# Strassen's seven products for the way up of two couples of blocks in the second MoE of a fused attention and MoE kernel

## The chip, the cores and the metric

One Trainium2 chip, one core of it. The metric is the device time of one execution in microseconds (us), the median of several runs.

## The reference

Attention with a causal mask and a forget bias feeds a gated MoE of one expert, and its result a second one; no step between them leaves the chip. What the change touches is the second:

```python
def _moe2_ref(x, w_in, w_out):      # x: 2304 x 512, w_in: 512 x 2048, w_out: 2048 x 512
    h = x @ w_in
    g = h - np.tanh(h)
    return (g @ w_out).astype(np.float32)
```

All of it is float32. The kernel keeps that precision on float16 operands: each operand is split into a high half (float16) and a low half (the rest, float16), and a product is three matmuls, high by high, high by low and low by high (`mm3`).

## The kernel before, in words

The 2304 tokens are cut into 6 blocks of 384 (`NBLK`, `TB`). Attention runs first, the first MoE of block j beside the attention of the next, and then the second MoE alone, block after block: for j in 0 to 5, 16 slices of 128 hidden columns on the way up (`up2`), then 4 parts of 128 output columns on the way down (`down2`). A slice on the way up is 4 pieces of 128 inputs by `mm3`, so 12 matmuls of 128 x 128 by 128 x 384, into one PSUM tile of `mm_tile` (4 of them in turn, tag `m2`). Then ScalarE takes the tanh (L1114), VectorE the difference of h and tanh h (L1115, which frees the PSUM tile), ScalarE copies it into the high half `DH` (L1116), and VectorE makes the low half `DL` (L1117). A part on the way down is 16 pieces by `mm3`, 48 matmuls, then an eviction on ScalarE (L1128) and a store.

The matmuls of all of them are the lines of `mm3`: L681, L682, L683. Weights come as 64-bit words that VectorE turns into float32 (`decode`, L547 to L549), ScalarE squares for their scale (L238), and `split` turns into halves (L563 on ScalarE, L564 on VectorE). These steps are a list of tasks (`w2_tasks`), run bit by bit in the last block of the first MoE and in block 0 of the second. A block's input is loaded as `x2f` and made into halves `x2h`, `x2l` by `x2_prep` (L1068, L1078, L1079).

The order on each engine is not the order of the code: the tile framework's scheduler moves instructions of one engine past each other where their data allow. On an engine they then run strictly in that order. `st_m1`, `st_m2` and the like are stacks of pools, closed when their memory goes to another.

Of the kernel before, what the change touches and what calls it, by code (L numbers as in the profile page):

```python
# [21 lines left out]
NBLK = 6  # L22
# [18 lines left out]
def tile_forget_attention_moe_moe2(ctx, tc, qa, qb, kt, va, vb, va0, vb0, s, wg, wv, wo, rg, win, wo2, out):  # L41
# [61 lines left out]
        return p.tile([128, 512], dtype, name=tag, tag=tag)  # L103

    wide = [None]

    def mm_tile():
# [878 lines left out]
    wide[0] = ps_x  # L986
# [4 lines left out]
    wt2 = {}  # L991

    def w2_tasks():
# [41 lines left out]
        def o_chain(g):
            ps = ps_x.tile([128, 512], FP32, name="px", tag="px")
            ones_sum(ps, wt2["ss"], 4)
            nm = small(const, [128, 1], FP32, f"nmo{g}")
            V.tensor_reduce(out=nm, in_=ps[:, 0:4], op=ALU.add, axis=AX.X)
            p2(nm, iso[:, g:g + 1], so[:, g:g + 1])  # L1040

        def o_conv(g, k):
            split(W2, 4 * g + k, so[:, g:g + 1])

        for key, piece, chain, conv in (("i", in_piece, in_chain, in_conv), ("o", o_piece, o_chain, o_conv)):
            for g in range(4):
                for k in range(4):
                    tasks.append(lambda g=g, k=k, piece=piece: piece(g, k))
                tasks.append(lambda g=g, chain=chain: chain(g))
                for k in range(4):  # L1050
                    tasks.append(lambda g=g, k=k, conv=conv: conv(g, k))
            if key == "i":
                tasks.append(lambda: V.tensor_reduce(out=wt2["si"], in_=si, op=ALU.min, axis=AX.X))
        return tasks

    x2s = {}

    def x2_load(j):
        t = x2_p.tile([128, 4, TB], FP32, name="x2f", tag="x2f", bufs=1)
        SY.dma_start(out=t, in_=x2d[j])  # L1060
        x2s[j] = t

    def x2_prep(j):
        t = x2s.pop(j)
        xh = x2_p.tile([128, 4, TB], FP16, name="x2h", tag="x2h")
        xl = x2_p.tile([128, 4, TB], FP16, name="x2l", tag="x2l")
# [10 lines left out]
        V.reciprocal(out=isd, in_=sd)  # L1077
        A.activation(out=xh, in_=t, func=ACTF.Copy, scale=sx)  # L1078
# [23 lines left out]

    st_m2 = ctx.enter_context(ExitStack())
    d_p = pool(st_m2, "d", bufs=1)
    t2_p = pool(st_m2, "t2", bufs=4)
    def up2(j, f, DH, DL):
        xh, xl, u, sd, _ = x2s[j, "p"]
        o = slice(128 * (f % 4), 128 * (f % 4) + 128)
        ps = mm_tile()
        for k in range(4):  # L1110
            mm3(ps, slot_h(WI, 4 * (f // 4) + k)[:, o], slot_l(WI, 4 * (f // 4) + k)[:, o], xh[:, k, :], xl[:, k, :], k, k == 0, k == 3)
        flush_moe()
        t = t2_p.tile([128, TB], FP32, name="t2", tag="t2")
        A.activation(out=t, in_=ps, func=ACTF.Tanh, scale=u[:, f // 4:f // 4 + 1])  # L1114
        V.scalar_tensor_tensor(out=t, in0=ps, scalar=u[:, f // 4:f // 4 + 1], in1=t, op0=ALU.mult, op1=ALU.subtract)  # L1115
        A.activation(out=DH[:, f, :], in_=t, func=ACTF.Copy, scale=sd)  # L1116
        moe_pend.append(lambda: V.scalar_tensor_tensor(out=DL[:, f, :], in0=t, scalar=sd, in1=DH[:, f, :], op0=ALU.mult, op1=ALU.subtract))  # L1117

    def down2(j, d, DH, DL):
# [4 lines left out]
        for k in range(16):  # L1124
            n, o = 4 * d + k // 4, slice(128 * (k % 4), 128 * (k % 4) + 128)
            mm3(ps, slot_h(W2, n)[:, o], slot_l(W2, n)[:, o], DH[:, k, :], DL[:, k, :], k, k == 0, k == 15)
        t = t2_p.tile([128, TB], FP32, name="t2", tag="t2")
        A.activation(out=t, in_=ps, func=ACTF.Copy, scale=io)  # L1128
        SY.dma_start(out=out[j, d], in_=t)

    for j in range(NBLK):
        DH = d_p.tile([128, 16, TB], FP16, name="dh", tag="dh")
        DL = d_p.tile([128, 16, TB], FP16, name="dl", tag="dl")
        for f in range(16):
            up2(j, f, DH, DL)
            if j == 0:
                run_tasks(w2t, -(-(nt - n5) // 14))
        if j == 0:
            run_tasks(w2t, 1000)
            st_ws.close()  # L1140
        if j + 1 < NBLK:
            x2_prep(j + 1)
            if j + 2 < NBLK:
                x2_load(j + 2)
        for d in range(4):
            down2(j, d, DH, DL)
    for st in (st_m2, st_w2):
        st.close()


# [49 lines left out]
```

## Time and profile before

| | |
|---|---|
| runs of the kernel | 1079.31, 1079.76, 1075.13 us; median 1079.31 |
| profiled execution | 1077.7 us, its span 1076.0 us |
| TensorE | busy 986.0 us, 92% of the span |
| VectorE, ScalarE, GpSimd | 621.3, 606.5 and 268.9 us |
| mean granted TensorE clock | 0.978 of 2.4 GHz |

In the profile PE is TensorE's matmuls, PEld its loads of weights, DVE VectorE, ACT ScalarE, POOL GpSimd and SP the engine that issues the DMAs. PEclk is the granted clock, 1.00 for 2.4 GHz. Matmuls overlap in their pipeline, so their durations add up to more than the time they take; the distance from one start to the next is what one costs. L1115 is line 1115 of the kernel before; the lines of the changed one are higher (L1254 there is L1115 here, L1256 is L1117, L1128 became L1269).

### The profile page before, as it was taken

The page shows a single profiled execution, that of the slowest core. Times are in us where ns is not written, and L with a number is a line of the kernel's source. Part 1 is how long each engine was busy: PE and PEld are TensorE (multiplying, and loading weights), DVE is VectorE, ACT ScalarE, POOL GpSimd, SP SyncE. Part 2 cuts the span into 40 slices and gives each one's busy share as a digit, 9 for nine tenths or more (in the row PEclk, how much of TensorE's full clock was granted, in tenths as well). Part 3 has the DMA queues.
Part 4 walks back from the last instruction along what each step waited for, and adds up shares of the span by engine and source line. Part 5 has one row for each costly group of instructions (what it writes and reads, how often), then busy time and mean ns, then how long its engine had stood idle before and what let it go on. Part 6 is the DMA issues. An engine that isn't in the chain of part 4 may idle for free.

```text
span 1076.0 us, 19457 instructions
## 1 busy us (share of the span) xinstructions
PE 986.0 (92%) x7575; PEld 626.7 (58%) x7576; DVE 621.3 (58%) x1445; ACT 606.5 (56%) x1194; POOL 268.9 (25%) x377
## 2 busy tenths in 40 slices
PE   1488977799899999999999899999999999999998
PEld 1376644455566666666666556666666666666665
DVE  8987998975585640673453988395442606243250
ACT  6589667776665662867667456465442516243240
POOL 5121265513462451455355112000000000000000
PEclk9986979999999999999999999999999999999999
DMA  8615524240202201301101950141010010100000
GB/s 271 251 36 123 177 87 125 64 140 30 66 22 60 54 17 67 90 12 27 55 12 39 339 172 13 48 156 45 16 37 23 5 55 2 45 15 9 23 1 30
DMA packets 49439, 76.82 MB, mean 71 GB/s; under 512 B 25890, under 2 KB 35202, under 8 KB 48834
## 3 DMA queue, kind: packets, MB, share of 16 engines
q1 hardware_dynamic: 49346, 75.58, 22.6%
q8 instruction: 59, 0.97, 0.4%
q14 instruction: 34, 0.28, 0.1%
HBM read 59.42 MB, written 9.55 MB: 64 GB/s over the span
## 4 chain that ended last, share of the span: by engine, by line
PE 70%; DVE 13%; DMA 8%; ACT 4%; issue 3%; POOL 2%; SPq 1%; ACTq 0%; DVEq 0%; POOLq 0%
PE m L681 13%; PE m L683 13%; PE m L682 13%; PE mm L681 7%; PE mm L683 7%; PE mm L682 7%; PE pv L482 2%; PE st L440 1%; PE st L441 1%; DMA wo<-wg 1%; DMA w<-wo 1%; DVE r L405 1%; DVE tm L699 1%; DVE q L356 1%; PE pv L486 1%
## 5 line engine op out<-in xcount | busy, mean ns | idle before, releaser
L681 PE MATMUL mm<-xth,w 128*128 128x384 f16 x480 | 159.3, 332 | 25.0 <-DVE tm L699 17.8
L682 PE MATMUL mm<-xtl,w 128*128 128x384 f16 x480 | 159.0, 331 | 0.4 <-DMA xtl<-xl 0.4
L683 PE MATMUL mm<-xth,w 128*128 128x384 f16 x480 | 158.4, 331 | 0.1
L682 PEld LDWEIGHTS <-w 128*128 128x128 f16 x960 | 94.5, 98 | 83.5 <-issue 29.6
L1115 DVE SCALAR_TENSOR_TENSOR t<-m,u,t 128x384 f32<-128x384 f32 x96 | 59.1, 616 | 140.1 <-ACT t L1114 137.7
L683 PEld LDWEIGHTS <-w 128*128 128x128 f16 x960 | 94.2, 98 | 63.1 <-issue 3.0
L681 PEld LDWEIGHTS <-w 128*128 128x128 f16 x960 | 95.3, 99 | 61.2 <-issue 2.8
L683 PE MATMUL m<-x2h,wi 128*128 128x384 f16 x384 | 125.2, 326 | 0.0
L682 PE MATMUL m<-x2l,wi 128*128 128x384 f16 x384 | 125.2, 326 | 0.0
L681 PE MATMUL m<-x2h,wi 128*128 128x384 f16 x384 | 125.2, 326 | 0.0
L683 PE MATMUL m<-dh,w 128*128 128x384 f16 x384 | 125.2, 326 | 0.0
L682 PE MATMUL m<-dl,w 128*128 128x384 f16 x384 | 125.2, 326 | 0.0
L681 PE MATMUL m<-dh,w 128*128 128x384 f16 x384 | 125.2, 326 | 0.0
L462 POOL TENSOR_TENSOR phl<-pf,phl 128x512 f16<-128x512 f32 (+2 forms) x90 | 97.7, 1093 | 40.7 <-ACT phl L455 39.5
L710 POOL TENSOR_TENSOR sl<-tm,sh 128x384 f16<-128x384 f32 x72 | 73.3, 1018 | 110.1 <-ACT sh L709 108.8
L1122 POOL TENSOR_SCALAR io<-iso,isd 128x1 f32<-128x1 f32 x24 | 6.6, 274 | 375.7 <-ACT t L1128 365.4
L1116 ACT ACTIVATE dh<-t,sd 128x384 f16<-128x384 f32 x96 | 59.0, 615 | 61.1 <-DVE t L1115 60.8
L1128 ACT ACTIVATE t<-m,io 128x384 f32<-128x384 f32 x24 | 13.9, 580 | 140.3 <-PE m L683 140.3
L1117 DVE SCALAR_TENSOR_TENSOR dl<-t,sd,dh 128x384 f16<-128x384 f32 x96 | 59.1, 616 | 52.7 <-ACT dh L1116 51.9
L450 POOL TENSOR_SCALAR_AFFINE_SELECT pf<-pf 128x128 f32<-128x128 f32 (+3 forms) x105 | 43.5, 417 | 176.3 <-ACT pf L448 175.8
L448 ACT ACTIVATE pf<-st,lnp,ilam 128x512 f32<-128x512 f32 (+2 forms) x105 | 73.2, 704 | 25.4 <-PE st L441 17.9
L681 PE MATMUL mm<-sh,wo 128*128 128x384 f16 x240 | 77.9, 326 | 2.3 <-DVE tm L699 2.3
(314 smaller groups left out, 2281.7 us busy)
## 6 DMA issues: line engine op xcount, KB each, us to landing
raw<-wo SPq DMA_DIRECT2D x16, 512.0 KB
w<-win SPq DMA_DIRECT2D x16, 512.0 KB
wo<-wg SPq DMA_DIRECT2D x12, 512.0 KB
wo<-wv SPq DMA_DIRECT2D x12, 512.0 KB
stk<-kt SPq DMA_DIRECT2D x4, 1152.0 KB
x2d<-tm SPq DMA_DIRECT2D x24, 192.0 KB
x2f<-x2d SPq DMA_DIRECT2D x6, 768.0 KB
out<-t SPq DMA_DIRECT2D x24, 192.0 KB
```

The lines of the kernel that those rows point to most:

```text
L448: A.activation(out=pf[:, 0:o], in_=ps[:, 0:o], func=ACTF.Exp, scale=bstate[b]["ilam"][:, hh:hh + 1], bias=lnp)
L450: G.affine_select(out=dg, in_=dg, pattern=[[0, len(heads)], [1, w]], compare_op=ALU.is_ge, fill=0.0, base=0, channel_multiplier=-1)
L462: G.tensor_tensor(out=u["pl"][:, 0:n], in0=u["pf"][:, 0:n], in1=u["ph"][:, 0:n], op=ALU.subtract)
L482: P.matmul(out=ps[0:w, o:o + 65], lhsT=u["pf"][:, cs], rhs=vs.bitcast(FP32), start=(c == 0), stop=(c == nch - 1))
L681: P.matmul(out=ps, lhsT=wh, rhs=xh, start=first, stop=False)
L682: P.matmul(out=ps, lhsT=wh, rhs=xl, start=False, stop=False)
L683: P.matmul(out=ps, lhsT=wl, rhs=xh, start=False, stop=last)
L710: moe_pend.append(lambda: G.tensor_tensor(out=SH["l"][:, f, :], in0=t, in1=SH["h"][:, f, :], op=ALU.subtract))
L1115: V.scalar_tensor_tensor(out=t, in0=ps, scalar=u[:, f // 4:f // 4 + 1], in1=t, op0=ALU.mult, op1=ALU.subtract)
L1116: A.activation(out=DH[:, f, :], in_=t, func=ACTF.Copy, scale=sd)
L1117: moe_pend.append(lambda: V.scalar_tensor_tensor(out=DL[:, f, :], in0=t, scalar=sd, in1=DH[:, f, :], op0=ALU.mult, op1=ALU.subtract))
L1128: A.activation(out=t, in_=ps, func=ACTF.Copy, scale=io)
```

## The change

Blocks 2 and 3, and 4 and 5, are couples. With x of two blocks as B (two halves of the inputs by two blocks) and `w_in` as a 2 x 2 matrix of quarters (halves of the inputs by halves of the hidden columns), the way up of a couple is one 2 x 2 product by Strassen's algorithm in Winograd's form: seven products of quarters in place of eight. `pair_up` makes it in 8 slices, each with 7 products of 2 pieces by `mm3`, 42 matmuls. Four scaled sums on VectorE (`add`) put the products together into the four results `c`, and `rest`, called twice with two results each (768 columns), takes tanh, difference, high and low half; its last step, the low half, is on GpSimd (`by`), in the last slice on VectorE.

For this the quarters of `w_in` that share a column half get one common scale (`in_chain` over 8 pieces), and four sums of quarters are made: S1, S2, S4 by `three` into a new tile `SF` during block 1, and S3 by `fourth` in place of quarter 21 after it. `x2_forms` makes the seven operand forms of x of a couple, in place of two `x2_prep`. From block 2 on the four banks of `m2` are two tiles of two banks (`mm_pair`): the way down takes its tiles as halves of them. The store of `DH` and `DL` is now one tile for four blocks' halves, and the way down of a couple goes through the pieces as the slices finish them.

```diff
@@ mm_tile
-        if wide[0] is not None:
+        if wide[0] is not None and not pairs[0]:
             return wide[0].tile([128, 512], FP32, name="m2", tag="m2", bufs=4)[:, 0:TB]
+        if pairs[0]:
+            if not half:
+                pair = mm_pair()
+                half.extend(pair[:, i, 0:TB] for i in range(2))
+            return half.pop(0)
@@ w2_tasks
-        for key, piece, chain, conv in (("i", in_piece, in_chain, in_conv), ("o", o_piece, o_chain, o_conv)):
-            for g in range(4):
...
+        for g in range(2):
+            for gg in (g, g + 2):
                 for k in range(4):
...
+                    tasks.append(lambda gg=gg, k=k: in_piece(gg, k))
+            tasks.append(lambda g=g: in_chain(g))
@@ x2_forms
+        for i, t in enumerate((a, b)):
+            A.activation(out=xf[:, i].rearrange("p a k t -> p (a k) t"), in_=t, func=ACTF.Square, accum_out=ss[:, i:i + 1])
...
+        def form(i, t):
+            A.activation(out=xf[:, i, 0], in_=t, func=ACTF.Copy, scale=sx)
+            V.scalar_tensor_tensor(out=xf[:, i, 1], in0=t, scalar=sx, in1=xf[:, i, 0], op0=ALU.mult, op1=ALU.subtract)
...
@@ form_tasks
+        def put(q, g, k, t):
+            h, l = halves_of(q, g, k)
+            A.activation(out=h, in_=t, func=ACTF.Copy)
+            V.tensor_tensor(out=l, in0=t, in1=h, op=ALU.subtract)
+
+        def three(g, k):
...
+            V.tensor_tensor(out=t, in0=l21, in1=l22, op=ALU.add)
+            V.tensor_tensor(out=t, in0=t, in1=h21, op=ALU.add)
+            V.tensor_tensor(out=t, in0=t, in1=h22, op=ALU.add)
+            put("S1", g, k, t)
+            V.tensor_tensor(out=w, in0=t, in1=l11, op=ALU.subtract)
+            V.tensor_tensor(out=w, in0=w, in1=h11, op=ALU.subtract)
+            put("S2", g, k, w)
...
@@ pair_up
+        def product(ps, q, form, s8):
+            g, o = s8 // 4, slice(128 * (s8 % 4), 128 * (s8 % 4) + 128)
+            for k in range(2):
+                h, l = wf["of"](q, g, k)
+                mm3(ps[:, 0:TB], h[:, o], l[:, o], xf[:, form, 0, k, :], xf[:, form, 1, k, :], k, k == 0, k == 1)
+
+        def rest(c, s8, a, z, by):
+            ds = slice(a, a + z + 1, z)
+            t = t2_p.tile([128, 2, TB], FP32, name="ta", tag="ta", bufs=2)
+            A.activation(out=t, in_=c[:, ds], func=ACTF.Tanh, scale=isd)
+            V.scalar_tensor_tensor(out=c[:, ds], in0=t, scalar=nsd, in1=c[:, ds], op0=ALU.mult, op1=ALU.add)
+            A.activation(out=DH[:, s8, ds, :], in_=c[:, ds], func=ACTF.Copy)
+            by.tensor_tensor(out=DL[:, s8, ds, :], in0=c[:, ds], in1=DH[:, s8, ds, :], op=ALU.subtract)
...
+            product(m1, "11", B11, s8)
+            A.activation(out=s1[:, 0], in_=m1[:, 0:TB], func=ACTF.Copy, scale=sg)
+            product(m26[:, 0], "12", B21, s8)
+            product(m26[:, 1], "S2", T2, s8)
+            add(c[:, 0:2], m26[:, :, 0:TB], s1.to_broadcast([128, 2, TB]))
+            product(m7, "S3", T3, s8)
+            add(c[:, 2], m7[:, 0:TB], c[:, 1])
+            product(m5, "S1", T1, s8)
+            add(c[:, 1:4:2], m5[:, 0:TB].unsqueeze(1).to_broadcast([128, 2, TB]), c[:, 1:3])
+            product(m34[:, 0], "S4", B22, s8)
+            product(m34[:, 1], "22", T4, s8)
+            rest(c, s8, 0, 3, V if s8 == 7 else G)
+            add(c[:, 1:3], m34[:, :, 0:TB], c[:, 1:3])
+            rest(c, s8, 1, 1, V if s8 == 7 else G)
```

Three places of the order as built follow. First VectorE in the last third of block 0's way up, before (`t` is a slice's tile, `m` its product, `dl` the low half; L1039 and L1002 to L1005 belong to the scale of the down weights):

```order
L1115 SCALAR_TENSOR_TENSOR t_9418<-m_9404,u_8768,t_9418 128x384
L1117 SCALAR_TENSOR_TENSOR dl<-t_9382,sd,dh 128x384
L1003 TENSOR_SCALAR iso<-iso 128x1
L1117 SCALAR_TENSOR_TENSOR dl<-t_9400,sd,dh 128x384
L1115 SCALAR_TENSOR_TENSOR t_9436<-m_9422,u_8768,t_9436 128x384
L1004 TENSOR_SCALAR iso<-iso 128x1
L1117 SCALAR_TENSOR_TENSOR dl<-t_9418,sd,dh 128x384
L1115 SCALAR_TENSOR_TENSOR t_9454<-m_9440,u_8768,t_9454 128x384
```

And the same place now (L1254 and L1256 are the difference and the low half, `sf` and `sft` the sums of weights, `xf` their working space):

```order
L1203 TENSOR_TENSOR sft<-wi 128x512
L1256 SCALAR_TENSOR_TENSOR dl<-t_9389,sd,dh 128x384
L1180 TENSOR_TENSOR sf<-xf,sf 128x512 x2
L1204 TENSOR_TENSOR sft<-sft,wi 128x512
L1060 TENSOR_REDUCE nmo_9307<-px 128x1
L1180 TENSOR_TENSOR sf<-xf,sf 128x512
L131 TENSOR_SCALAR x2e<-px 128x1
L1180 TENSOR_TENSOR sf<-xf,sf 128x512
L1188 TENSOR_TENSOR xf<-wi 128x512
L1180 TENSOR_TENSOR sf<-xf,sf 128x512
L1254 SCALAR_TENSOR_TENSOR t_9425<-m_9411,u_8743,t_9425 128x384
```

Rows of 512 columns from `three` and `fourth` now stand between one slice's difference and the next.

Second, VectorE in block 2's way up, before:

```order
L1115 SCALAR_TENSOR_TENSOR t_10493<-m_10479,u_10017,t_10493 128x384
L1117 SCALAR_TENSOR_TENSOR dl<-t_10493,sd,dh 128x384
L1115 SCALAR_TENSOR_TENSOR t_10511<-m_10497,u_10017,t_10511 128x384
L1117 SCALAR_TENSOR_TENSOR dl<-t_10511,sd,dh 128x384
L119 TENSOR_SCALAR x2e<-px 128x1
L1115 SCALAR_TENSOR_TENSOR t_10529<-m_10515,u_10017,t_10529 128x384
```

And now, the first slices of the couple of blocks 2 and 3 (L1300 is `add`, L1287 the difference in `rest`, `c` a slice's results, `m`, `mm` and `px` its products):

```order
L1300 SCALAR_TENSOR_TENSOR c_10339<-m_10337,sigma,c_10340 128x768
L1300 SCALAR_TENSOR_TENSOR c_10339<-mm,sigma,c_10339 128x384
L1300 SCALAR_TENSOR_TENSOR c_10339<-px,sigma,c_10339 128x2x384
L1300 SCALAR_TENSOR_TENSOR c_10339<-m_10338,sigma,c_10339 128x768
L1287 SCALAR_TENSOR_TENSOR c_10339<-ta,nsd,c_10339 128x2x384
L1300 SCALAR_TENSOR_TENSOR c_10403<-m_10401,sigma,c_10404 128x768
L1287 SCALAR_TENSOR_TENSOR c_10339<-ta,nsd,c_10339 128x768
L1300 SCALAR_TENSOR_TENSOR c_10403<-mm,sigma,c_10403 128x384
```

The fourth sum has gone ahead of the first difference, and the next slice's first sum stands between a slice's two differences: so at four of the seven handovers of this couple (behind slices 0, 1, 2 and 6).

Third, VectorE at a handover of the couple of blocks 4 and 5, now:

```order
L1300 SCALAR_TENSOR_TENSOR c_11316<-m_11315,sigma,c_11316 128x768
L1287 SCALAR_TENSOR_TENSOR c_11316<-ta,nsd,c_11316 128x2x384
L1287 SCALAR_TENSOR_TENSOR c_11316<-ta,nsd,c_11316 128x768
L1300 SCALAR_TENSOR_TENSOR c_11380<-m_11378,sigma,c_11381 128x768
L1300 SCALAR_TENSOR_TENSOR c_11380<-mm,sigma,c_11380 128x384
```

Here both differences stand together, at all seven handovers.

## Rows read from the trace of the kernel before

**Rows 1.** The page: busy time of TensorE, and its slices with the clock.
```profile
PE 986.0 (92%) x7575; PEld 626.7 (58%) x7576; DVE 621.3 (58%) x1445; ACT 606.5 (56%) x1194; POOL 268.9 (25%) x377
...
PE   1488977799899999999999899999999999999998
...
PEclk9986979999999999999999999999999999999999
```

**Rows 2.** Windows: busy time by engine in the stretch, with counts; then clock, DMA.
```profile
738.00:1049.00 311.00, 311.00 (x1920) 187.74 (x1919) 112.02 (x196) 121.36 (x195) 5.17 (x19) 1.00 0.07 24
```

**Rows 3.** Timeline of TensorE from 879.78: start, duration, engine, line.
```profile
879.78 0.33 PE L682 MATMUL m<-dl,w 128*128 128x384 f16 x1
...
888.88 0.33 PE L681 MATMUL m<-x2h,wi 128*128 128x384 f16 x1
```

**Rows 4.** Groups by line and form, VectorE: busy us, mean ns; idle before.
```profile
L1117 DVE SCALAR_TENSOR_TENSOR dl<-t,sd,dh 128x384 f16<-128x384 f32 x96 | 59.1, 616 | 52.7 <-ACT dh L1116 51.9 <-PE m L683 0.7
L1115 DVE SCALAR_TENSOR_TENSOR t<-m,u,t 128x384 f32<-128x384 f32 x96 | 59.1, 616 | 140.1 <-ACT t L1114 137.7
...
L1079 DVE SCALAR_TENSOR_TENSOR x2l<-x2f,x2s,x2h 128x1536 f16<-128x1536 f32 x6 | 10.9, 1818 | 3.9 <-ACT x2h L1078 3.9
```

**Rows 5.** The same view, ScalarE.
```profile
L1116 ACT ACTIVATE dh<-t,sd 128x384 f16<-128x384 f32 x96 | 59.0, 615 | 61.1 <-DVE t L1115 60.8
L1114 ACT ACTIVATE t<-m,u 128x384 f32<-128x384 f32 x96 | 55.7, 580 | 13.7 <-PE m L683 8.2 <-DVE dl L1117 0.3
...
L1078 ACT ACTIVATE x2h<-x2f,x2s 128x1536 f16<-128x1536 f32 x6 | 9.4, 1562 | 0.3 <-DVE x2s L123 0.3
...
L1068 ACT ACTIVATE x2l<-x2f 128x1536 f16<-128x1536 f32 x6 | 8.9, 1482 | 4.0 <-DMA x2f<-x2d 3.9
```

**Rows 6.** The same view, GpSimd.
```profile
L710 POOL TENSOR_TENSOR sl<-tm,sh 128x384 f16<-128x384 f32 x72 | 73.3, 1018 | 110.1 <-ACT sh L709 108.8
L462 POOL TENSOR_TENSOR phl<-pf,phl 128x512 f16<-128x512 f32 x42 | 52.5, 1259 | 23.0 <-ACT phl L455 22.8
```

**Rows 7.** Timeline of VectorE and GpSimd around 299.6 and 473.
```profile
299.35 0.16 DVE L532 SCALAR_TENSOR_TENSOR ss<-ss 128x1 f32<-128x1 f32 x1
...
299.86 0.89 DVE L532 SCALAR_TENSOR_TENSOR ss<-ss 128x1 f32<-128x1 f32 x1
...
299.58 1.16 POOL L462 TENSOR_TENSOR phl<-pf,phl 128x512 f16<-128x512 f32 x1 [0.23 <-ACT phl L455]
...
473.10 0.55 DVE L708 SCALAR_TENSOR_TENSOR tm<-tm,mm 128x384 f32<-128x384 f32 x1 [0.53 <-PE mm L683]
...
472.46 1.81 POOL L306 TENSOR_SCALAR vt<-stv,vs 128x512 f16<-128x512 f32 x3 [0.85 <-DVE vs L123]
```

**Rows 8.** Windows over block 0 of the second MoE, columns as in rows 2.
```profile
697.00:705.00 8.00, 8.00 (x52) 4.83 (x50) 3.54 (x7) 3.55 (x6) 0.00 (x0) 1.00 0.73 254
705.00:729.00 24.00, 24.00 (x151) 14.62 (x150) 24.00 (x50) 18.02 (x40) 0.00 (x0) 1.00 0.30 100
729.00:737.00 8.00, 8.00 (x53) 4.96 (x53) 7.28 (x23) 6.06 (x9) 0.00 (x0) 1.00 0.00 0
737.00:760.00 23.00, 23.00 (x143) 13.88 (x142) 3.65 (x5) 5.69 (x9) 0.96 (x3) 1.00 0.18 61
```

**Rows 9.** Timeline of VectorE in block 0's way up; idle time before in brackets.
```profile
701.07 0.62 DVE L1117 SCALAR_TENSOR_TENSOR dl<-t,sd,dh 128x384 f16<-128x384 f32 x1 [0.68 <-ACT dh L1116]
...
703.28 0.43 DVE L547 TENSOR_SCALAR w<-raw 128x512 int32<-128x512 int32 x1 [0.94 <-DMA raw<-wo]
...
715.59 0.68 DVE L549 SCALAR_TENSOR_TENSOR w<-raw,w 128x512 int32<-128x512 int32 x1
716.20 0.60 DVE L1117 SCALAR_TENSOR_TENSOR dl<-t,sd,dh 128x384 f16<-128x384 f32 x1
```

**Rows 10.** Timeline, the last matmul and the last eviction.
```profile
1072.29 0.33 PE L683 MATMUL m<-dh,w 128*128 128x384 f16 x1
1072.70 0.58 ACT L1128 ACTIVATE t<-m,io 128x384 f32<-128x384 f32 x1 [7.21 <-PE m L683]
```

More of the change, by code (lines that the diff above doesn't have):

```diff
@@ L985, in tile_forget_attention_moe_moe2 @@
     ps_x = pool(st_w2, "ps_x", bufs=2, side="right", space=PSUM)
-    wide[0] = ps_x
+    st_pm = ctx.enter_context(ExitStack())
+    wide[0] = pool(st_pm, "ps_m2", side="right", space=PSUM)
     x2_p = pool(st_w2, "x2", bufs=2, side="right")
@@ L991, in tile_forget_attention_moe_moe2, with wi_slot @@
     wt2 = {}
+    def wi_slot(g, k):
+        return 4 * (2 * (g % 2) + g // 2) + k
     def w2_tasks():
@@ L1050, in w2_tasks @@
                 for k in range(4):
[L1051 to L1054, printed above, removed]
+                    tasks.append(lambda gg=gg, k=k: in_conv(gg, k))
+        tasks.append(in_last)
+        n_in = len(tasks)
+        for g in range(4):
+            for k in range(4):
+                tasks.append(lambda g=g, k=k: o_piece(g, k))
+            tasks.append(lambda g=g: o_chain(g))
+            for k in range(4):
+                tasks.append(lambda g=g, k=k: o_conv(g, k))
@@ L1077, in x2_prep @@
         V.reciprocal(out=isd, in_=sd)
+        return isx, sx, sd, isd
+    def x2_prep(j):
+        t = x2s.pop(j)
+        if j == 0:
+            xx = x2_p.tile([128, 4, TB], FP32, name="x2f", tag="x2f").rearrange("p k t -> p (k t)").bitcast(FP16).rearrange("p (a k t) -> p a k t", a=2, k=4)
+            xh, xl = xx[:, 0], xx[:, 1]
+        else:
+            xh, xl = (XF[0][:, 5 + i].rearrange("p a k t -> p (a k) t") for i in range(2))
+        ss = small(sc_p, [128, 1], FP32, "ssx")
+        A.activation(out=xl, in_=t, func=ACTF.Square, accum_out=ss)
+        isx, sx, sd, isd = x2_scale(ss, 1)
+        u = small(sc_p, [128, 4], FP32, "u2")
+        V.tensor_scalar(out=u, in0=wt2["isi"], scalar1=isx, scalar2=None, op0=ALU.mult)
         A.activation(out=xh, in_=t, func=ACTF.Copy, scale=sx)
@@ L1123, in down2 @@
         ps = mm_tile()
-        for k in range(16):
+        order = [f for s8 in range(8) for f in (s8, s8 + 8)] if j > 1 else list(range(16))
+        for i, k in enumerate(order):
+            a, z = d_at(j, k)
             n, o = 4 * d + k // 4, slice(128 * (k % 4), 128 * (k % 4) + 128)
-            mm3(ps, slot_h(W2, n)[:, o], slot_l(W2, n)[:, o], DH[:, k, :], DL[:, k, :], k, k == 0, k == 15)
+            mm3(ps, slot_h(W2, n)[:, o], slot_l(W2, n)[:, o], DH[:, a, z, :], DL[:, a, z, :], k, i == 0, i == 15)
         t = t2_p.tile([128, TB], FP32, name="t2", tag="t2")
@@ new lines, in tile_forget_attention_moe_moe2 @@
+    st_sf = ctx.enter_context(ExitStack())
+    three = fourth = []
+    for j in range(NBLK):
+        if j == 1:
+            three, fourth = form_tasks(st_sf)
+        if j < 2:
+            for f in range(16):
+                up2(j, f)
+                if j == 0:
+                    run_tasks(w2t, -(-(nt - n5) // 14))
+                elif f % 4 == 1:
+                    run_tasks(three, 1)
+        elif j % 2 == 0:
+            if j == 2:
+                st_pm.close()
+                wide[0] = pool(st_pm, "ps_mp", side="right", space=PSUM)
+                pairs[0] = bool(1)
+            pair_up(j)
@@ L1140, in tile_forget_attention_moe_moe2 @@
             st_ws.close()
[L1141 to L1144, printed above, removed]
+            x2_prep(1)
+            x2_load(2)
+            x2_load(3)
+        elif j < NBLK - 1:
+            if j % 2:
+                run_tasks(fourth, 4)
+                x2_forms(j + 1)
+            if j % 2 and j + 3 < NBLK:
+                x2_load(j + 3)
+                x2_load(j + 4)
         for d in range(4):
-            down2(j, d, DH, DL)
-    for st in (st_m2, st_w2):
+            down2(j, d)
+    for st in (st_pm, st_sf, st_m2, st_w2):
         st.close()
```

164 lines of the change are left out of this document (119 added, 45 removed).

## The prediction

> **What bounds the kernel now.** I began with the whole program: TensorE is busy 986.0 of 1076.0 us and its row in the slices stays at 8 or 9 behind the first tenth, with the clock at 9 tenths or more almost throughout [rows 1]. Such a share could still hide waits, so I went to the stage that the change touches. In the 311 us from 738 to 1049, which hold blocks 1 to 4 of the second MoE nearly whole, TensorE is busy for all 311.00 us at a granted clock of 1.00, that is, at the 2.4 GHz level; VectorE is busy for 112, ScalarE for 121 and GpSimd for 5 [rows 2]. Nothing but the number of matmuls sets the end there. What one costs is the distance between starts, not the duration of its row: 57 rows in sequence start from 879.78 to 888.88, so 9.10 / 56 = 0.1625 us each, while a row lasts 0.33 because two overlap [rows 3].
>
> **What is removed.** Before, a block's way up has 16 slices of 12 matmuls, so a couple of blocks has 384. The change makes 8 slices of seven products of 6 matmuls, 336 in all. Two couples save 96 matmuls of the same form: 96 x 0.1625 = **15.6 us**, all on the path that sets the end. The rest of the sum is what the added work takes back from this.
>
> **The couples' seven products.** One new slice of 42 matmuls lasts 42 x 0.1625 = 6.83 us on TensorE. Beside it VectorE has four sums (three over 768 columns, one over 384) and two differences over 768. No row of before has 768 columns. Its bounds: from 384 columns (616 ns) to 1536 (1818 ns) a column costs 1202 / 1152 = 1.043 ns, which gives 616 + 384 x 1.043 = 1017 ns; two of the 384 form would be 1232 ns [rows 4]. I take 1017, since one instruction runs over both banks. VectorE then needs 5 x 1.017 + 0.616 = 5.70 us of 6.83. ScalarE, by the same step (615 at 384, 1562 at 1536: 931 ns at 768), needs 0.58 + 4 x 0.931 = 4.30 us [rows 5]. GpSimd, which did nothing here before, gets two subtractions over 768 columns: by the mean rows, 1018 ns at 384 and 1259 at 512, the slope gives 1.74 us and doubling 2.04 [rows 6]; I take 1.9, so 3.8 us. Each engine fits, VectorE with 1.13 us to spare.
>
> Two things eat this reserve. VectorE and GpSimd stand in each other's way: at 299.86 a VectorE instruction over a single column, with two SBUF inputs, lasts 0.89 us where the same line took 0.16 half a microsecond earlier, and it ends at 300.75, just as the GpSimd subtraction of 299.58 to 300.74 ends. One that has an input in PSUM is not held: 0.55 us at 473.10 in the middle of GpSimd's 472.46 to 474.27 [rows 7]. So the four sums run free, the two differences (`rest`, both inputs in SBUF) can be held. In the order as built they mostly stand side by side, after the last sum; GpSimd's work starts only behind the copy that follows the first difference, and has 6.83 - 2 x 1.02 = 4.79 us until the next pair of them for its 3.8. In the first couple, however, four of the seven handovers have the next slice's first sum between the two differences: up to 4 x 1.9 = 7.6 us of holding. Also ScalarE's two squares for the next couple (1.48 us each [rows 5], with 0.2 for the accumulator) stand in slices 6 and 7 of the first. Against this are 8 x 1.13 = 9.0 us of reserve and the banks: the first pair of banks is emptied about 4.0 us into a slice (18 matmuls, 2.93, and a sum, 1.02) and written again at 6.83 + 0.98 = 7.8, so VectorE may be 3.8 us late before TensorE notices. Bounds: 0 and 7.6; I take **1.0 us**, most of it where the first couple's way down meets its last slice.
>
> **The weight sums in block 0.** The sums of weights (`three`, `fourth`: 56 VectorE instructions over 512 columns and 16 ScalarE copies) are written into block 1, but the order as built draws a good part forward. Between the first and the last of the 16 products' differences of block 0, VectorE now has 19 more rows of 512 columns. A row of that size starts 0.61 us after the one before it (715.59 to 716.20 [rows 9]), so 19 x 0.60 = 11.4 us. Before, VectorE was without a pause in just that place: 24.00 of 24.00 us from 705 to 729, 7.28 of the next 8, and only behind 737 idle (3.65 of 23) [rows 8]. Its pauses after the start, 0.68 and 0.94 us [rows 9], take 1.6. What remains, 9.8, delays the differences that empty PSUM; TensorE has four tiles, so it runs ahead by three slices of 12 x 0.1625 = 1.95 us, 5.85, before it waits. 9.8 - 5.85 = **4.0 us** of waiting, with 0 and 9.8 as bounds (0 if ScalarE's copies let the rows slip, 9.8 if TensorE's lead is already used up). The splits of the last two parts of the down weights stand behind these rows too; they are needed two parts later, over 15 us on.
>
> **The tail and the rest.** With coupled banks the second half of a tile waits until the first half is emptied. Elsewhere other parts' matmuls were moved between; for the last part of block 5 none is left: an eviction ends 1072.70 + 0.58 - 1072.29 = 0.99 us after the start of the last matmul before it [rows 10], where the next matmul otherwise starts after 0.16, so **0.8 us**. The operand forms of a couple (per couple 7 differences and 4 subtractions over 768, 11 x 1.02 = 11.2 us) and `fourth` lie in ways down of 4 x 7.8 = 31 us, where VectorE did 3.65 us in 23 [rows 8]: nothing. Grouping `w_in` by eight pieces leaves the same decodes, squares and splits: nothing, with 3 us as the bound, since TensorE is full there as well. The two x2 loads in place of one have over 30 us to land: nothing.
>
> **Sum.** -15.6 + 1.0 + 4.0 + 0.8 = -9.8 us. The profiled execution took 1077.7 us (span 1076.0), so 1067.9. It lies 1.6 under the median of the runs and near their mean of 1078.1; I forecast **1068**.
>
> **The rivals.** *Everything is covered.* TensorE's lead takes the block 0 rows, and the couples lose nothing: 1077.7 - 15.6 + 0.8 = 1063. For it speaks that the lead and the pauses are at least 7.4 of the 11.4 us; against, the 24 full microseconds. *Two banks cost twice.* If a sum over two banks costs 1232 ns, VectorE needs 5 x 1.232 + 0.616 = 6.78 of 6.83 us and has no reserve. The first couple then pays its 7.6 and the squares' 3.3 less the 3.8 of lateness, 7.1, and the second some 0.1 to 0.2 a slice, 1: -15.6 + 8.1 + 4.0 + 0.8 = -2.7, 1075, which cannot be told from no change. *VectorE and GpSimd take turns (slower).* If each difference meets a running GpSimd subtraction in every slice, VectorE's time is 5.70 + 3.8 = 9.5 us, 2.67 over TensorE's, in 16 slices: 42.7 us, and the sum is -15.6 + 42.7 + 4.8 = +31.9, 1110. It decides from 1.13 + 10.8 / 16 = 1.8 us of holding per slice on, one whole GpSimd row: below that the kernel is still not slower. For it speaks the 0.89 us row [rows 7]; against, that only 4 of 14 handovers are interleaved and that the two differences come together ahead of the copies that start GpSimd.
>
> The Trainium skill, page "SBUF — State Buffer", section "Who interferes with whom", has a rule against this change: a VectorE instruction with two SBUF inputs contends with a GpSimd instruction that reads SBUF, and whichever issues second is blocked until the first has finished. By that rule, where GpSimd is always first, the time is that of this last rival; the trace agrees that the holding is whole, with the 0.89 us row, but no run here shows yet who comes first in the couples.
>
> **How the numbers follow.** My forecast has a chance of 0.60 (its own range 1063 to 1074, from the bounds of block 0), the covered case 0.17, two banks 0.14, taking turns 0.09. What a measurement of this kernel can tell from no change is about 0.5%, 5.4 us, so the first two are faster, the third the same, the last slower: 0.77, 0.14, 0.09. The range reaches down to 1061.5 (the covered case, with the scatter of the runs) and up to 1077, over the third case; it leaves out the fourth and the ends.
>
> **What would show it.** Right: rows of 768 columns at about 1.02 us on VectorE; TensorE full at a clock of 1.00 in both ways up of couples, each about 55 us; pauses of TensorE of 0.3 to 2 us in block 0, put down to the difference line on VectorE; one of 0.8 us some 8 us before the last matmul. Wrong: block 0 without pauses (the covered case), 768-column rows over 1.2 us, TensorE waiting regularly for VectorE in the couples with differences of 2 us and more, or waits at the start of the first couple for its operand forms, which I cost at nothing.

## The result, and the profile after

The changed kernel takes 1068.06 us (median of 5 runs, 1065.54 to 1070.69) against 1079.31 us before (5 runs, 1075.13 to 1079.76). The ratio is 0.9904, with a 95% interval of 0.9876 to 0.9932: faster by 0.7 to 1.2%. The profiled execution took 1068.06 us, its span is 1066.3 (before 1076.0), so the spans differ by 9.7 us. The medians differ by 11.3, since the profiled execution of the kernel before lies 1.6 us under its median; below, the spans are explained.

The lines are now those of the changed kernel: `mm3` is L693 to L695, the difference of a single block L1254, a sum of products L1300, the difference in `rest` L1287, its copy L1288 and its low half L1289.

The page of the changed kernel first: busy time by engine, and two rows of the slices.

```profile
PE 973.4 (91%) x7472; PEld 616.0 (58%) x7472; DVE 679.9 (64%) x1472; ACT 606.6 (57%) x1172; POOL 320.6 (30%) x405
...
PE   1488878799899999999999899999999999999998
...
PEclk9977988999999999999999999999999999999999
```

Beside [rows 1], TensorE has 12.6 us less of busy time while VectorE has 59 and GpSimd 52 more. (7575 - 7472 = 103 rows of matmuls fewer: the 96, 8 small sums for scales, and one other row more.)

The windows of the changed kernel: four over block 0, as in [rows 8], and one over the end of each couple's way up. Columns: stretch and length, then busy time and instructions of TensorE, its loads, VectorE, ScalarE, GpSimd; clock, DMA share, GB/s.

```profile
697.00:705.00 8.00, 8.00 (x51) 4.83 (x50) 5.96 (x10) 3.82 (x7) 0.00 (x0) 1.00 0.33 99
705.00:729.00 24.00, 21.24 (x130) 12.42 (x129) 22.99 (x46) 14.78 (x31) 0.00 (x0) 1.00 0.43 151
729.00:737.00 8.00, 8.00 (x52) 4.94 (x51) 8.00 (x19) 7.63 (x16) 0.00 (x0) 1.00 0.28 83
737.00:760.00 23.00, 23.00 (x143) 13.81 (x142) 22.22 (x45) 12.62 (x20) 5.75 (x2) 1.00 0.17 59
...
835.00:893.00 58.00, 58.00 (x359) 34.87 (x358) 48.69 (x50) 34.19 (x43) 24.77 (x15) 1.00 0.01 3
940.00:998.00 58.00, 58.00 (x359) 34.88 (x357) 40.31 (x44) 27.98 (x36) 22.31 (x15) 1.00 0.01 4
```

In the couples TensorE is full at the 2.4 GHz level: 58.00 of 58. In block 0 it now lacks 2.76 of 24 us, where [rows 8] had 24.00. Who it waited for, from 598 us (the last block of the first MoE) to the end (total us, times, longest):

```profile
PE m L693 <- DVE tm L711: 3.1, 2, 2.5
PE m L693 <- DVE t L1254: 2.2, 3, 0.9
PE mm L693 <- DVE tm L711: 1.4, 1, 1.4
PE m L693 <- ACT t L1269: 0.7, 1, 0.7
PE m L693 <- DVE iso L1020: 0.6, 1, 0.6
```

The last of these lines names the wrong instruction: `iso` only stands next to the difference that TensorE waits for.

```profile
727.02 0.61 DVE L1254 SCALAR_TENSOR_TENSOR t<-m,u,t 128x384 f32<-128x384 f32 x1
727.54 0.14 DVE L1020 TENSOR_SCALAR iso<-nmo 128x1 int32<-128x1 int32 x1
...
727.68 0.32 PE L693 MATMUL m<-x2f,wi 128*128 128x384 f16 x1 [0.55 <-DVE iso L1020]
```

The matmul starts 0.05 us behind the end of the difference (727.63), as at the three other waits, and not behind the end of `iso` (727.68); it belongs to block 0's way up, which does not use that scale. So all four waits in block 0 are for the difference.

No line names a sum or difference of the couples (L1300, L1287) or a low half (L1289). These are their groups from 820 us on (busy us, mean ns, then idle time before), first VectorE's, then ScalarE's, then GpSimd's:

```profile
L1287 DVE SCALAR_TENSOR_TENSOR c<-ta,nsd,c 128x768 f32<-128x768 f32 x32 | 35.6, 1114 | 4.2 <-ACT ta L1286 4.0
L1300 DVE SCALAR_TENSOR_TENSOR c<-m,sigma,c 128x768 f32<-128x768 f32 x32 | 32.5, 1015 | 57.3 <-PE m L695 55.6
L1300 DVE SCALAR_TENSOR_TENSOR c<-mm,sigma,c 128x384 f32<-128x384 f32 x16 | 9.8, 616 | 9.1 <-PE mm L695 7.7 <-DVE c L1300 0.5
...
L1286 ACT ACTIVATE ta<-c,isd 128x768 f32<-128x768 f32 x32 | 29.8, 932 | 29.9 <-DVE c L1300 29.9
L1288 ACT ACTIVATE dh<-c 128x768 f16<-128x768 f32 x32 | 26.8, 839 | 8.7 <-DVE c L1287 8.6
...
L1289 POOL TENSOR_TENSOR dl<-c,dh 128x768 f16<-128x768 f32 x28 | 48.0, 1730 | 54.9 <-ACT dh L1288 54.9
```

A sum that reads both coupled PSUM banks in one instruction takes 1015 ns, twice the 384 form less 217.

To add up where the time went I take TensorE's pauses: the distance between the starts of two neighbouring matmuls, less 0.1625 us (less for the small sums of scales, by their columns), wherever 0.03 us or more is left. A pause comes out about 0.16 us longer than the idle time in brackets, since neighbouring rows overlap. The first MoE up to about 572 us is untouched by the change, but a row found in both kernels there (a sum of the first MoE, 572.13 before) starts at 572.84, 0.7 later.

| stretch, us | pauses before | pauses after |
|---|---|---|
| 598 to 698, last block of the first MoE | 4.85 | 5.92 |
| 698 to 832, blocks 0 and 1 | 0.62 | 4.21 |
| 832 to the last matmul | 0.40 | 1.01 |

That is +1.1, +3.6 and +0.6 (0.88 in the tail, less 0.27 for two pairs of small sums that are gone). With -15.6 for the matmuls it makes -10.3; with the 0.7 of the untouched part -9.6, against a measured -9.7.

### The profile page after: what moved, and what is told of

Its sections match the earlier page's. It is cut to its first block, busy times and chain, and to the rows that moved or that the text cites. A ratio compares the mean times of both kernels' runs of the same rounds, so it can differ in the third digit from the quotient of the medians.

```text
span 1066.3 us, 19297 instructions
## 1 busy us (share of the span) xinstructions
PE 973.4 (91%) x7472; PEld 616.0 (58%) x7472; DVE 679.9 (64%) x1472; ACT 606.6 (57%) x1172; POOL 320.6 (30%) x405
## 4 chain that ended last, share of the span: by engine, by line
PE 62%; DVE 18%; DMA 8%; ACT 5%; issue 4%; POOL 1%; SPq 1%; ACTq 0%; DVEq 0%; POOLq 0%
PE m L693 10%; PE m L695 10%; PE m L694 10%; PE mm L693 8%; PE mm L695 8%; PE mm L694 8%; DMA stv<-qb 1%; DVE w L560 1%; PE st L452 1%; PE st L453 1%; DMA raw<-wo 1%; DVE tm L711 1%; DMA w<-wo 1%; PE pv L494 1%; DVE r L417 1%
## 5 line engine op out<-in xcount | busy, mean ns | idle before, releaser
L693 PE MATMUL mm<-xth,w 128*128 128x384 f16 x480 | 161.3, 336 | 24.3 <-DVE tm L711 18.2
L695 PE MATMUL mm<-xth,w 128*128 128x384 f16 x480 | 160.4, 335 | 0.1
L695 PEld LDWEIGHTS <-w 128*128 128x128 f16 x960 | 94.7, 99 | 64.8 <-issue 5.0
L693 PEld LDWEIGHTS <-w 128*128 128x128 f16 x960 | 95.3, 99 | 62.2 <-issue 4.0
L693 PE MATMUL m<-dh,w 128*128 128x384 f16 x384 | 124.1, 326 | 0.7 <-ACT t L1269 0.7
L695 PE MATMUL m<-dh,w 128*128 128x384 f16 x384 | 124.1, 326 | 0.0
L722 POOL TENSOR_TENSOR sl<-tm,sh 128x384 f16<-128x384 f32 x72 | 76.2, 1059 | 112.9 <-ACT sh L721 103.7
L1261 POOL TENSOR_SCALAR io<-iso,isd 128x1 f32<-128x1 f32 x24 | 12.0, 501 | 257.1 <-ACT t L1269 257.1
L1269 ACT ACTIVATE t<-m,io 128x384 f32<-128x384 f32 x24 | 13.8, 578 | 126.7 <-PE m L695 123.0
L693 PE MATMUL mm<-sh,wo 128*128 128x384 f16 x240 | 78.0, 326 | 2.3 <-DVE tm L711 2.3
L695 PE MATMUL mm<-sh,wo 128*128 128x384 f16 x240 | 78.2, 326 | 0.7 <-DVE wo L576 0.7
L694 PE MATMUL mm<-sl,wo 128*128 128x384 f16 x240 | 78.1, 326 | 0.0
L452 PE MATMUL st<-q,kl 128*128 128x128 f16 (+1 forms) x456 | 62.5, 216 | 9.1 <-DVE q L368 2.7
L1300 DVE SCALAR_TENSOR_TENSOR c<-m,sigma,c 128x768 f32<-128x768 f32 x32 | 32.5, 1015 | 57.3 <-PE m L695 55.6
L1289 POOL TENSOR_TENSOR dl<-c,dh 128x768 f16<-128x768 f32 x28 | 48.0, 1730 | 54.9 <-ACT dh L1288 54.9
L711 DVE SCALAR_TENSOR_TENSOR tm<-tm,mm 128x384 f32<-128x384 f32 x60 | 32.9, 548 | 43.9 <-ACT tm L710 41.4
```

The costliest lines, as they stand in the source:

```text
L452: P.matmul(out=ps[:, o:o + w], lhsT=K2[sl][:, ks], rhs=q2_of(T)[:, h, 0:w], start=True, stop=False)
L693: P.matmul(out=ps, lhsT=wh, rhs=xh, start=first, stop=False)
L694: P.matmul(out=ps, lhsT=wh, rhs=xl, start=False, stop=False)
L695: P.matmul(out=ps, lhsT=wl, rhs=xh, start=False, stop=last)
L711: V.scalar_tensor_tensor(out=t, in0=t, scalar=1.0, in1=ps, op0=ALU.add, op1=ALU.mult)
L722: moe_pend.append(lambda: G.tensor_tensor(out=SH["l"][:, f, :], in0=t, in1=SH["h"][:, f, :], op=ALU.subtract))
```

## The experiments

Each ratio is taken against runs of the kernel before on the same chip: median 1079.06 us (15 runs, 1074.42 to 1083.39) for the eighth product, the low halves, the doubled subtractions and the regrouping, 1077.93 (9 runs, 1076.21 to 1079.52) for the other three. The executions of one kernel lie 3 to 9 us apart, so terms of 1 to 3 us are read from the pauses, and spans are compared from the same row near 572 us on.

**The price of a product on the path.** One of the seven products is made twice in each slice:

```diff
             product(m1, "11", B11, s8)
+            product(m1, "11", B11, s8)
```

> The first product of every slice is made twice, so a couple's slice has 48 matmuls again, as two plain slices of four blocks would. My theory (TensorE alone sets the end in the couples, everything else is covered): 16 slices x 6 matmuls x 0.1625 = 15.6 us more than the changed kernel, 1083.7, and so about 4.5 us over the kernel before: that is then what the change's added work costs. Rival (VectorE or the holding by GpSimd sets the pace of a slice, and the saved matmuls are only partly in the time): the added matmuls fall into waits that are there already, and less than 10 us are added.

It took 1085.18 us (6 runs, 1083.22 to 1086.14), ratio 1.0045 (1.0026 to 1.0064): 17 us over the change by the medians. Inside one trace each the size is sharper: the last matmul before the pause near the end starts at 1069.09 (in the change 1053.93) and the last sum of scales of block 1 at 770.63 (771.07), so the 96 added matmuls cost 15.16 + 0.44 = 15.6 us, 0.1625 each, and the pauses from 832 on are 1.01 us as in the change. A matmul is worth its whole price, in either direction. With it what the added work costs shows alone, 1085.18 - 1079.06 = 6.1 us: with eight products the change is slower than the kernel before.

**The weight sums of block 0.** `three` and `fourth` do the same work, but are placed behind the last difference of block 0 (`mark` is that instruction):

```diff
-                    run_tasks(three, 1)
+                    with tc.issue_after(mark[0]):
+                        run_tasks(three, 1)
...
+            mark[0] = [i for i in nc.cur_bb.bb.instructions if i.engine == last_r[0].engine][-1]
...
-                run_tasks(fourth, 4)
+                with tc.issue_after(mark[0]):
+                    run_tasks(fourth, 4)
```

> VectorE's rows of the weight sums are queued behind the last difference of block 0's way up, so that none is drawn into it. My theory (the 19 drawn rows are what TensorE waits for in block 0, 3.6 us): TensorE's pauses between 699 and 735 us fall from 4.2 to 1.5 us or less, the ways down of block 0 and the way up of block 1 take the rows without a pause, and the median falls by 2 to 3.6 us, to about 1065. Rival (the pauses come from the down weights that VectorE must take in there anyway, or the rows only move the pause into block 1): no difference beyond 1 us.

It took 1064.75 us (4 runs, 1063.95 to 1066.87), ratio 0.988 (0.9866 to 0.9894), an interval that overlaps that of the change; the size is read from the pauses. Its window over block 0, and its waits there:

```profile
705.00:729.00 24.00, 23.43 (x147) 14.20 (x145) 23.96 (x51) 17.19 (x38) 0.00 (x0) 1.00 0.40 135
...
PE m L693 <- DVE t L1254: 0.6, 1, 0.6
```

The pauses of 698 to 832 fall from 4.21 to 1.50 us, and from the row near 572 on the span is 490.0 us against 493.5 (0.7 of these 3.5 lie in 598 to 698, which the edit doesn't touch). The four other profiles that leave the sums in place have 4.3 to 4.9 us there. So 2.7 of the 3.6 us in block 0 come from the weight sums that the scheduler draws forward. The other 0.9 is left as it is: one wait for a difference (0.71) and small steps.

**The tail.** The halves of a way down come alternately from two coupled tiles:

```diff
-                pair = mm_pair()
-                half.extend(pair[:, i, 0:TB] for i in range(2))
+                two = [mm_pair() for _ in range(2)]
+                half.extend(two[i % 2][:, i // 2, 0:TB] for i in range(4))
```

> The ways down take the four halves of the two coupled tiles in turn (first halves of both, then second halves), so that the halves of one tile are never filled one straight after the other. My theory: the pause of 0.88 us before the last part is gone, and nothing else changes: 0.7 to 0.9 us less, within what can be told apart in the time, but plain in the trace. Rival (the pause is the store's tile or the scale that is waited for, not the half): the pause stays.

In the change, around the last coupled tile (start, duration, engine, line; idle time before in brackets):

```profile
1053.93 0.33 PE L695 MATMUL m<-dh,w 128*128 128x384 f16 x1
...
1054.34 0.58 ACT L1269 ACTIVATE t<-m,io 128x384 f32<-128x384 f32 x1 [3.48 <-PE m L695]
...
1054.97 0.32 PE L693 MATMUL m<-dh,w 128*128 128x384 f16 x1 [0.72 <-ACT t L1269]
```

1054.97 - 1053.93 - 0.16 = 0.88 us. In the experiment this pause is gone, and TensorE waits for nobody behind 832 us (0.13 us of pauses in all). The time is 1068.35 us (4 runs, 1065.46 to 1069.85), ratio 0.9902 (0.9884 to 0.9919): a gain of 0.9 us can't be told from none by the time. The trace shows the mechanism; the runs don't show its worth.

**Both edits at once.** The edits of the last two.

> Both edits together: the weight sums queued behind block 0's way up, and the halves in turn. If both theories hold the two add up: 3 to 4.4 us less than the changed kernel, 1063.7 to 1065, the fastest of all. Otherwise no better than the better of the two alone.

It took 1065.25 us (5 runs, 1061.01 to 1066.81), ratio 0.9873 (0.9853 to 0.9894), not to be told from the weight sums held back alone. The pauses behave as in the parts (1.27 and 0.13 us). What its profile has beyond them lies in 598 to 698, where neither edit reaches: 7.7 us of pauses against 5.2 with the weight sums held back alone, 1.6 of it in a stretch at the lower clock near 644 us (last section).

**Who holds whom.** First the rows of the change in the first couple, VectorE and GpSimd:

```profile
840.51 1.64 POOL L1289 TENSOR_TENSOR dl<-c,dh 128x768 f16<-128x768 f32 x1 [8.65 <-ACT dh L1288]
840.59 2.38 DVE L1287 SCALAR_TENSOR_TENSOR c<-ta,nsd,c 128x768 f32<-128x768 f32 x1
...
847.48 1.01 DVE L1287 SCALAR_TENSOR_TENSOR c<-ta,nsd,c 128x768 f32<-128x768 f32 x1
847.59 2.41 POOL L1289 TENSOR_TENSOR dl<-c,dh 128x768 f16<-128x768 f32 x1 [2.01 <-ACT dh L1288]
```

At 840.51 GpSimd is first, and the difference issued 0.08 us behind it lasts 2.38 us, to 842.97, 0.82 past GpSimd's end at 842.15. At 847.48 VectorE is first, and it is GpSimd that lasts 2.41 instead of 1.64. Whichever is second is held until the first has finished. In the second couple VectorE is always first, and none of its differences lasts longer than 1.02 us:

```profile
961.15 1.02 DVE L1287 SCALAR_TENSOR_TENSOR c<-ta,nsd,c 128x768 f32<-128x768 f32 x1 [0.47 <-ACT ta L1286]
961.93 3.35 POOL L1289 TENSOR_TENSOR dl<-c,dh 128x768 f16<-128x768 f32 x2 [3.48 <-ACT dh L1288]
```

In the change a difference lasts 1114 ns in the mean and a sum 1015, so all holding of VectorE is 32 x 0.099 = 3.2 us, nearly all of it in the first couple (its rows at 840.59 and 883.49, of 2.38 and 2.42, make 2.8 of it).

To force the holding, each of GpSimd's subtractions is made twice:

```diff
             by.tensor_tensor(out=DL[:, s8, ds, :], in0=c[:, ds], in1=DH[:, s8, ds, :], op=ALU.subtract)
+            if by is G:
+                by.tensor_tensor(out=DL[:, s8, ds, :], in0=c[:, ds], in1=DH[:, s8, ds, :], op=ALU.subtract)
```

> Every low half that GpSimd makes in the couples is made twice there. The theory of an exclusive hold (a VectorE instruction with two SBUF inputs and a GpSimd instruction that reads SBUF never run at once): GpSimd's four runs of 1.73 us and VectorE's two differences of 1.02 us must follow each other, 8.95 us a slice against 6.83, 2.1 us over in 14 slices, 30 us, less the lateness that the banks allow (up to 3.8 per couple): 1090 to 1098, slower than the kernel before. Rival (no hold, each engine at its own pace): GpSimd has 6.92 us a slice, 0.1 over TensorE, and the time stays within 2 us of the changed kernel.

It took 1080.97 us (10 runs, 1077.96 to 1083.64), ratio 1.0017 (0.9999 to 1.0036): 13 us over the change, between the two expectations. The groups of the differences and of both subtractions (L1291 is the added one), then TensorE's waits from 832 us on:

```profile
L1287 DVE SCALAR_TENSOR_TENSOR c<-ta,nsd,c 128x768 f32<-128x768 f32 x32 | 59.4, 1885 | 0.7 <-ACT ta L1286 0.7
...
L1291 POOL TENSOR_TENSOR dl<-c,dh 128x768 f16<-128x768 f32 x28 | 56.5, 2036 | 0.3
L1289 POOL TENSOR_TENSOR dl<-c,dh 128x768 f16<-128x768 f32 x28 | 53.5, 1926 | 14.3 <-ACT dh L1288 14.3
...
PE m L693 <- DVE c L1302: 8.6, 8, 1.8
PE m L694 <- DVE dl L1289: 1.4, 3, 0.6
```

A difference now lasts 1885 ns, and the 32 of them are held for 59.4 - 32 x 1.015 = 26.9 us, 1.9 us in each of the 14 slices with GpSimd. TensorE's pauses from 832 on rise from 1.01 to 13.27 us. The rest of the holding costs it nothing. The holding is as real as its theory had it, and GpSimd is held too (1.93 and 2.04 us in place of 1.65); the expectation was too high by its sizes. In the first couple four of TensorE's waits end 7.85 us apart (858.68, 866.53, 874.37, 882.22), and meanwhile GpSimd has no pause and VectorE none over 0.1 us. GpSimd's subtractions start 1.60 us apart, and two of the four, held by a difference, 0.71 later: 4 x 1.60 + 2 x 0.71 = 7.8. The expectation had 4 x 1.73 + 2 x 1.02 = 8.95, with durations in place of start distances. GpSimd's doubled work alone, 4 x 1.60 = 6.4 us, would fit into TensorE's 6.83, so it is the holding that costs.

**No GpSimd at all.** VectorE makes the low halves of every slice:

```diff
-            rest(c, s8, 0, 3, V if s8 == 7 else G)
+            rest(c, s8, 0, 3, V)
...
-            rest(c, s8, 1, 1, V if s8 == 7 else G)
+            rest(c, s8, 1, 1, V)
```

> All low halves of the couples are made on VectorE, none on GpSimd. My theory (VectorE has a reserve of about 1.1 us a slice and is not held in practice): VectorE needs 5.70 + 2 x 0.96 = 7.6 us a slice against TensorE's 6.83, is 6.3 us late at the end of a couple, of which the banks allow 3.8, so some 2 to 3 us per couple and 1070 to 1074 in all (4 to 6 us over the changed kernel). Rival (GpSimd's holding already takes the reserve, so taking GpSimd out gives back as much as the two subtractions cost): no difference within 1 us.

It took 1071.26 us (4 runs, 1069.48 to 1072.85), ratio 0.9919 (0.9897 to 0.9941). The interval overlaps that of the change. From the row near 572 on its span is 2.3 us longer, 1.6 of which are pauses from 832 on (2.60 against 1.01) and 0.6 in 598 to 698, which this edit doesn't touch. Of the 1.6, one wait for a sum of VectorE's makes 0.52 (at 997.40), and a second pause like that of the tail, with the same line waited for (L1269), makes 0.88 (at 1023.27). So the time doesn't show that GpSimd's share is worth anything, and by the trace it saves TensorE one wait of 0.5 us, much less than I had it. Its rows say why (VectorE):

```profile
963.13 1.02 DVE L1287 SCALAR_TENSOR_TENSOR c<-ta,nsd,c 128x768 f32<-128x768 f32 x1
964.07 1.01 DVE L1300 SCALAR_TENSOR_TENSOR c<-m,sigma,c 128x768 f32<-128x768 f32 x1
965.00 1.01 DVE L1287 SCALAR_TENSOR_TENSOR c<-ta,nsd,c 128x768 f32<-128x768 f32 x1
965.92 0.95 DVE L1289 TENSOR_TENSOR dl<-c,dh 128x768 f16<-128x768 f32 x1
966.79 0.61 DVE L1300 SCALAR_TENSOR_TENSOR c<-mm,sigma,c 128x384 f32<-128x384 f32 x1
```

A row of 768 columns lasts 1.02 us, but the next one starts 0.93 behind it, 0.87 behind a low half and 0.53 behind a row of 384 (the next is at 967.32): 5 x 0.93 + 2 x 0.87 + 0.53 = 6.9 us per slice, against 6.83 on TensorE. I had counted 7.6 by durations. Without GpSimd no difference is held either.

**The regrouping alone.** The kernel before with only the grouping of `w_in` by eight pieces:

```diff
+    def wi_slot(g, k):
+        return 4 * (2 * (g % 2) + g // 2) + k
...
-                wt2["ssi"] = small(const, [128, 4], FP32, f"ssi{g}")
+                wt2["ssi"] = small(const, [128, 8], FP32, f"ssi{g}")
...
+        for g in range(2):
+            for gg in (g, g + 2):
+                for k in range(4):
+                    tasks.append(lambda gg=gg, k=k: in_piece(gg, k))
+            tasks.append(lambda g=g: in_chain(g))
```

> The kernel before with one part of the change alone: the input weights' scales are made for two quarters of eight pieces each in place of four of four. My theory, from the two traces (TensorE's pauses in the last block of the first MoE add up to 5.9 us after and 4.9 before, both at products that wait for VectorE): this part costs 1 us, so TensorE's pauses between 598 and 698 us add up to about 5.9 us and the time is 1080. Rival (the difference is scatter of the DMAs): pauses as before, 4.9 us.

One run, 1081.63 us, inside the scatter of the kernel before. In its profile, from the row near 572 on, the span is 2.4 us longer than before, all of it in 598 to 698, where the pauses are 7.22 us against 4.85. One wait of VectorE's sums of the first MoE grows. Here is its end before, then in the change, then in this experiment:

```profile
641.72 0.32 PE L681 MATMUL m<-xth,w 128*128 128x384 f16 x1 [1.32 <-DVE tm L699]
```

```profile
643.36 0.32 PE L693 MATMUL m<-xth,w 128*128 128x384 f16 x1 [2.48 <-DVE tm L711]
```

```profile
644.10 0.47 PE L681 MATMUL m<-xth,w 128*128 128x384 f16 x1 [2.36 <-DVE tm L699]
644.36 0.53 PE L682 MATMUL m<-xtl,w 128*128 128x384 f16 x1
644.68 0.53 PE L683 MATMUL m<-xth,w 128*128 128x384 f16 x1
```

With the grouping that wait is longer, with or without the rest of the change: +1.0 us of pause in this run. In all nine profiles the same five rows of decoding stand between this sum of VectorE's and the one before it, so it is not more work that delays it. What differs here and in the change is how long VectorE waits for the weights of the first of the five: 0.78 and 0.83 us, against 0.25 before. Over the eight profiles with the grouping it is 0.06 to 1.07, and no run holds this load apart, so the cause stays argued. The other 1.3 us of this one execution go with a lower clock behind that wait (1.6 us, last section), less what the other pauses are shorter.

## Why the prediction held, point by point

**-15.6 us for 96 matmuls** held exactly. The eighth product puts the same number back and pays 15.6.

**+1.0 us for the couples** came out as 0. The parts of it were right: rows of 768 columns at 1015 to 1018 ns (taken as 1017), 932 on ScalarE (931), 1.73 us on GpSimd (1.9). VectorE was 5.52 us busy in the 6.82 of a slice of the second couple (predicted 5.70). Of the holding, bounded at 7.6 us, 3.2 came, in the first couple as the order of the instructions had it, and none of it reached TensorE. The step that was too careful is VectorE's need by durations: neighbouring rows start 0.93 us apart. The waits I feared at the start of a couple, for its operand forms, are not there.

**+4.0 us for the weight sums in block 0** came out as 3.6, in four waits of 0.53 to 0.93 us for the difference line, as forecast. Holding the sums back shows 2.7 us to be theirs. But the 19 rows that I counted are not the ones that cost. These rows of VectorE are weight sums of the change:

```profile
698.94 1.29 DVE L1188 TENSOR_TENSOR xf<-wi 128x512 f32<-128x512 f16 x2 [11.70 <-PE m L695]
...
712.64 0.68 DVE L1196 TENSOR_TENSOR xf<-xf,wi 128x512 f32<-128x512 f32 x1
...
732.77 0.67 DVE L1203 TENSOR_TENSOR sft<-wi 128x512 f32<-128x512 f16 x1
```

Twelve of them run from 698.94 to 713.3, ahead of the waits at 714 to 728; six of these stand before the first difference, and my count left them out. The other 13 of the 19 start only at 732.77, when the last pause is over. So the stage, the line and the sign were right, and that 4.0 came so near 3.6 is luck in part: by their place the rows that delay are 12 x 0.60 = 7.2 us early in block 0, not 11.4 over all of it. No run holds these twelve back alone.

Here is VectorE ahead of the longest of the four waits, and TensorE's row at its end:

```profile
722.87 0.43 DVE L559 TENSOR_SCALAR w<-raw 128x512 int32<-128x512 int32 x1 [0.44 <-DMA raw<-wo]
723.21 0.61 DVE L1256 SCALAR_TENSOR_TENSOR dl<-t,sd,dh 128x384 f16<-128x384 f32 x1
723.74 0.69 DVE L560 SCALAR_TENSOR_TENSOR w<-raw,w 128x512 int32<-128x512 int32 x1
724.35 0.61 DVE L1254 SCALAR_TENSOR_TENSOR t<-m,u,t 128x384 f32<-128x384 f32 x1
...
725.01 0.32 PE L693 MATMUL m<-x2f,wi 128*128 128x384 f16 x1 [0.93 <-DVE t L1254]
```

The difference that empties TensorE's bank stands behind a decode that itself waited 0.44 us for its weights. My working had only the added rows; a late load in the same queue adds to it.

**+0.8 us for the tail** came out as 0.88, and goes when the halves alternate.

**Nothing for the regrouping of `w_in`** is the term that was mis-sized: "the same decodes, squares and splits" is true, but one wait in the first MoE went from 1.48 to 2.64 us. The total, +1.1, lies inside the bound of 3 that I gave. In the eight profiles with this grouping that one wait's pause is 1.94 to 2.64 us. All the pauses of 598 to 698, without the rows at the lower clock, are 4.8 to 6.3, about 5.5 in the mean, against 4.85 in the only profile before: +0.7, with a scatter nearly as large. It hides in the sum since the couples came out 1.0 lower, so that the sum of -9.8 lies within 0.1 us of the measured spans is luck: two terms missed by about 1 us each, in opposite directions.

**The rivals.** *Everything is covered* was right for the couples and wrong for block 0. *Two banks cost twice* fell with the 1015 ns row. *Taking turns* had the right price and the wrong condition. Its point of decision was 1.8 us of holding per slice (1.9 if it is reckoned over the 14 slices that use GpSimd, in place of all 16). The doubled subtractions bring 1.9, and the time is 1.0017 of the kernel before, within its interval of no change. In the change as made it is 3.2 / 14 = 0.2 us, since the two differences of a slice mostly stand ahead of the copies that start GpSimd. The rule of the Trainium skill, page "SBUF — State Buffer", section "Who interferes with whom", that issue order decides who blocks, agrees with the rows at 840.51 and 847.59, one in each direction. It says nothing of who comes first here, and only the order of the instructions told that.

## What to carry to other kernels

Where TensorE is full, count matmuls by the distance between their starts and believe that number; then look for what the new work delays in the stages that were only just full on another engine. Here the couples' own sums cost nothing, and apart from the 0.88 us of the tail all that was given back came from VectorE's queue in stages ahead of them. In block 0 a scheduler had put work at the head of that queue that was not due for another 100 us (the first product with a weight sum starts behind 831). Whether two engines that lock each other out cost anything is read from the order of their instructions at each handover, and for the engine's need take start distances, not durations.

## What the runs showed of the hardware that I had not expected

VectorE's rows overlap: with 768 columns, a row lasts 1.02 us and the next starts 0.93 us after it; with 384 it is 0.61 and 0.53.

The lock between VectorE and GpSimd works in both directions, and holds GpSimd too: a subtraction of 1.64 us took 2.41 when a difference of 1.01 had started 0.11 us before it.

TensorE's clock can fall after a short pause in an otherwise full stretch. In the regrouping alone, TensorE paused for 2.53 us at 641.4, and the ten matmuls behind it start 0.32 us apart and last up to 0.53, until 647.6; that is 10 x 0.16 = 1.6 us more than at 2.4 GHz. The granted clock of these rows is 0.51, the 1.2 GHz level, and that of the 20 us around them 0.91:

```profile
644.10:647.50 3.40, 3.40 (x11) 1.61 (x11) 3.40 (x11) 2.87 (x9) 0.91 (x1) 0.51 0.00 0
640.00:660.00 20.00, 17.64 (x100) 10.18 (x99) 16.82 (x39) 12.61 (x26) 5.44 (x6) 0.91 0.04 14
```

The same window has 0.91 with both edits, without GpSimd and with the doubled subtractions (pauses of 2.33, 2.49 and 2.44 us at that place), but 1.00 in the change (2.64), with the eighth product (2.59), the halves in turn (2.33) and the sums held back (1.94). So the pause that the regrouping lengthens costs another 1.6 us or so in some executions and not in others, and its length alone does not say when (2.33 us with and without it). What decides it stays open.
